# One order for all loads behind the first batch's q and k, and two of its value copies moved to GpSimd

## The chip, the cores and the metric

The kernel runs on one core of one Trainium2 chip. The metric is the device time of one execution in microseconds (us), the median of several runs. The core has five engines that work side by side: TensorE (PE in the profile, with its weight loads as PEld), VectorE (DVE), ScalarE (ACT), GpSimd (POOL) and SyncE (SP). DMA engines carry the loads; here nearly all loads are issued from GpSimd's queue and the stores from SyncE's.

## What is computed

Sliding-window causal attention (window 64) over 8 batches, 8 heads, 576 positions and head size 64, followed by a two-layer feed-forward with SiLU:

```python
scores = scale * np.matmul(q, k.transpose(0, 1, 3, 2))
mask = (rel >= 0) & (rel < window)            # rel = i - j, window = 64
attn = softmax(np.where(mask, scores, -1e9))
attn_out = np.matmul(attn, v)                 # (8, 8, 576, 64)
x = attn_out.transpose(0, 2, 1, 3).reshape(4608, 512)
h = x @ w_in                                  # (512, 2048)
out = (h / (1 + exp(-h))) @ w_out             # (2048, 512)
```

Inputs and output are float32 in memory; the kernel computes in bfloat16 with float32 sums.

## The kernel before

**Attention.** A batch is done in three groups `g` of three windows of 64 queries. Each window sees 128 keys: its own block of 64 and the one before. Batch 0 is done in six units (three groups for each half `a` of the heads), the later ones in three units each. A unit is: scores on TensorE (`scores_first` for batch 0, L315 and L323, `scores` for the others, L335), exponentials on ScalarE (`expo`, L341), for later batches a mask on VectorE (`masking`, L344), the product with the values on TensorE (`values`, L353), then on VectorE the reciprocal of the sums (`inverse`, L360), the norm (`normal`, L363) and a transposition into `bridge` (`to_bridge`, L367), the tile from which the feed-forward reads.

**Loads.** Batch 0's q and k come in whole pairs of heads (`natb`, L234 and, for the first pair, L237) and are transposed on TensorE. For the other batches `load_rows` (L244) takes one head's q or k in a load of 72 KB, four to a buffer, and `turn_blocks` (L251) transposes a buffer on VectorE. `load_v` (L260) brings the values of two blocks of all heads, or of the last one; it fills the odd windows `n` of `vv`. The even ones are filled by `shift_v` (L301 and L303), which copies 64 partitions up or down, two copies for each of four parts. `load_w_in` (L263) brings w_in in ten pieces (four with 256 columns, six with 512, in pairs for the two halves `a` of the rows), `load_w_out` (L269) w_out in eight pieces of 256 rows.

**Feed-forward.** Nine tiles of 512 tokens. The first layer (`first_layer`, L373) goes through 16 weight tiles `ft` of 128 columns with four matmuls each, ScalarE applies SiLU (`silu`, L379), and the second layer (`second_layer`, L385) sums over the 16 in four banks of 128 tokens; `copy_out` (L391) and `store` end it. Tile 0 is special: its first layer takes 576 tokens, all of batch 0. For the first `THIRDS` weight tiles it works in widths of 192, one for each group of batch 0 (classes `in0`, `in1`, `in2`), so that it can begin when the first group is normed; for the others in widths of 256 and 320. Its second layer goes weight tile by weight tile, so that it needs w_out piece by piece. `rest_of_first` (L382) carries its last 64 tokens to tile 1. In tile 1 the first `SPLIT` weight tiles are done in two widths (192 and 256), the others in one (448). The score and value groups of a later batch are put between the matmuls of the second layer.

**What sets the order.** The class `Plan` runs a list of queues, one for each class of work (`dma`, `shift`, `norm`, ...). Each has a rank (tables `rank`, `rank0` for batch 0, `ahead` for its first group, `also`); a lower number goes first. `Plan.run` walks through time with a planned duration for each operation, and whenever an engine is free lets it take the head of the best queue whose inputs are ready. The order found in this way is written out as the program of each engine. All loads but batch 0's q and k are in the class `dma`, so they are issued from GpSimd in the order in which they were added: before, batch 0's values, all of w_in, then batch 1's q and k rows, w_out pieces and values in the order of `SECOND_LOADS`. A planned duration is not a measured one: on the chip each instruction waits for the semaphores of what it reads, and an engine goes through its program in order. GpSimd's loads use eight semaphores in turn, so a load waits for the landing of the one eight places before it.

While nothing can be done yet, TensorE runs filler matmuls on a blank tile (`warm`, L605).

Of the kernel before, what the change touches and what calls it, by code (L numbers as in the profile page):

```python
# [122 lines left out]
def kernel(ctx, tc, q, k, v, w_in, w_out, out):  # L123
# [14 lines left out]
    NN, NNB, NE, NOT, NGT = 8, 8, 12, 4, NFT + 3  # L138
    THIRDS, SPLIT, SECOND_LOADS = 4, 16, "0w12w3wvwvwvwvvww"
    FIRST_LOADS = [(x[0], int(x[1])) for x in "q0 k0 q1 k1 q2 q3 k2 k3 v0 v1 v2 v3 v4".split()]  # L140
    NOX, NRC, NV = 6, 6, 3
# [3 lines left out]
    def SHIFT(b, m, hf):  # L145
        return {"DVE": 0.31, **({"ACT": 0.64} if m > 1 else {})}
    scale = 1.0 / float(D) ** 0.5
# [34 lines left out]
        rank=dict(prime=-8, early=-10, one=-9, edge=-8.5, first=-9, dma=-1, ld0=-1, dma0=-8.7, st=-2, silu=-3, silu_in0=-3.1, silu_in1=-3.1, silu_in2=-3.1, silu_in3=-3, silu_next=-3, out=-2, pv=0, s=1, in0=96, in1=97, in2=98, in3=98.5, out0=98.7, next=98.9, moe=99, warm=200, turn=2,  # L182
                  norm=0, inverse=0, bridge=0, exp=1, mask=1, lift=2, block=2, shift=2, shift2=2, cast=4, rest=3, late=5, clear=9),
        rank0=dict(turn=-6, cast=-6, lift=-5, shift=-4.5, shift2=-4.05, exp=-4, mask=-4, inverse=-3.5, norm=-3, bridge=-3.2),
        ahead=dict(s=-6.5, exp=-4.6, pv=-5.5, inverse=-4.3, norm=-4.2, bridge=-4.25),
        also=dict(inverse1=-4.2, norm1=-4.1, bridge1=-4.15),
    )
# [230 lines left out]
    def add_first_batch():  # L418
        got = {}
        for what, u in FIRST_LOADS:  # L420
            if what == "v":
                add_v_loads(0, [u], [c_vv[0]])
                continue
            kk = "qk".index(what)
# [22 lines left out]
    def add_w_out(which):  # L447
        wout.extend(p.add("dma", {"POOL": 0.75}, lambda _, f=f: load_w_out(f), dma=1.29, lat=MARGIN) for f in which)

    def add_batch_qk(b):  # L450
        busy = s_last.get(b - NK, []) + ([c_k[b % NK]] if b < NK else [])
        for what in SECOND_LOADS if b < NIV else "0123":
            if what == "w":
                add_w_out([len(wout)])
            elif what == "v":
                add_v_loads(b, [len(v_landed.get(b, []))], [c_vv[b]])
            else:
                add_four(b, *divmod(int(what), 2), busy)

    def add_four(b, a, kk, busy):  # L460
        i = n_nat[0] % NN
        n_nat[0] += 1
        ld = [p.add("dma", {"POOL": 0.6}, lambda _, h=h: load_rows(i, b, a, kk, h), nat_free.get(i, []),
                    dma=0.42, lat=MARGIN) for h in range(4)]
        nat_free[i] = [p.add("block", {"DVE": 0.79}, lambda _, part=part: turn_blocks(i, b, a, kk, part),
                             ld + busy, b=b) for part in range(2)]
        kq_done[(b, a)] = kq_done.get((b, a), []) + nat_free[i]

    def add_v_loads(b, parts, busy):
        v_landed.setdefault(b, []).extend(  # L470
            p.add("dma", {"POOL": 1.0 if m < NPAIR else 0.75}, lambda e, m=m: load_v(e, b, m), busy,
                  dma=(0.95 if m < NPAIR else 0.5), lat=MARGIN * (b > 0)) for m in parts)

    def add_batch_v(b):
        busy = pv_last.get(b - NV, []) + [c_vv[b % NV]]
        if b >= NIV:
            add_v_loads(b, range(NPAIR + 1), busy)
        lv = v_landed[b]
        for g in range(NG):
            v_done[(b, g)] = lv[:g + 2] if g < 2 else list(lv)  # L480
        for m, z in ([(i, i + 1) for i in range(NPAIR)] if b < NIV else [(0, NPAIR)]):
            for hf in range(2):
                sh = p.add("shift" if b or 2 * m + hf < 3 else "shift2", SHIFT(b, m, hf) if b == 0 else {"DVE": 0.1 + 0.17 * (z - m)}, lambda e, hf=hf, m=m, z=z: shift_v(e, b, hf, m, z),
                           lv[m:z], b=b)
                for g in range(NG):
                    if any(3 * g <= n < 3 * g + 3 for n in range(2 * m + 2 * hf, 2 * z + 2 * hf, 2)):
                        v_done[(b, g)] = v_done[(b, g)] + [sh]
# [110 lines left out]


    add_first_batch()  # L600
    add_batch_v(0)


    def warm(op):
# [4 lines left out]
                 pool="all")  # L609
    for lo, hi in ((0, 256), (256, 512), (512, 1024), (1024, 1536), (1536, 2048)):  # L610
        landed = [p.add("dma", {"POOL": 0.6}, lambda _, a=a, lo=lo, hi=hi: load_w_in(a, lo, hi), dma=1.31 * (hi - lo) / 512)
                  for a in range(2)]
        win.extend([landed] * ((hi - lo) // 128))
    add_batch_attention(0)
# [4 lines left out]
    for b in range(1, B):  # L619
        add_batch_qk(b)  # L620
        add_batch_v(b)
        if b == 1:
            add_w_out(range(len(wout), 8))
        while TB * (n_tile + 1) <= b * NB:
            add_tile(n_tile)
            n_tile += 1
        add_batch_attention(b)
# [34 lines left out]
```

## Time and profile before

| what | value |
|---|---|
| median of 4 runs | 299.7 us (299.35 to 300.49) |
| the profiled execution | 300.49 us, span in the profile 298.7 us |
| TensorE busy | 290.8 us, 97% of the span, 3667 matmuls |
| ScalarE, VectorE, GpSimd busy | 177.1, 137.8, 118.9 us |
| granted TensorE clock | 1.00 throughout |
| DMA packets | 28.64 MB, mean 96 GB/s |

The span is what the profiler saw from the first instruction to the last; the time of a run is a little longer. "Busy" counts an engine's own instructions, on GpSimd also the time in which it writes the descriptors of a load (the `DMA_DIRECT2D` rows). In the timeline a row gives start, duration, engine, line, operation and count, and in brackets how long the engine was idle before and what ended that; "issue" there means that the profile shows nothing that it waited for. In the list of waits a row is engine, line, what it waited for, and the total, the number and the longest of the waits.

### The profile page before, as it was taken

The numbers are of one execution on the slowest core, as the hardware profiler recorded it, in microseconds if no ns is written. First come the engines' busy times: TensorE is split into PE (matmuls) and PEld (weight loads), VectorE is DVE, ScalarE is ACT, GpSimd is POOL, SyncE is SP. The second block draws the span as 40 slices with busy tenths as digits, with TensorE's granted clock in tenths as the row PEclk, the third lists the DMA queues.
The fourth block names the chain that finished last, engine by engine and source line by source line (L and its number), as shares of the span: only waits on it lengthen the run. The fifth ranks groups of instructions, "written<-read, shape, count | busy, mean of one in ns | idle before, by whom it ended". The sixth has DMA issues, their size and how long they took to land.

```text
span 298.7 us, 8593 instructions
## 1 busy us (share of the span) xinstructions
PE 290.8 (97%) x3667; PEld 151.4 (51%) x3667; DVE 137.8 (46%) x338; ACT 177.1 (59%) x348; POOL 118.9 (40%) x183
## 2 busy tenths in 40 slices
PE   8989979999999999999999999999999999999996
PEld 4568634885444544454444544454444544444444
DVE  4862448959985479327931692066006600000000
ACT  4888654886376745675477537753876376226511
POOL 8976976969999989953200000000000000000000
PEclk9999999999999999999999999999999999999999
DMA  8999999999999999986900210011001100011012
GB/s 165 173 188 166 138 170 163 226 135 135 170 183 143 128 186 178 150 82 104 122 0 1 72 53 22 2 41 68 35 2 37 72 35 3 35 70 37 0 70 71
DMA packets 83110, 28.64 MB, mean 96 GB/s; under 512 B 72576, under 2 KB 78336, under 8 KB 83072
## 3 DMA queue, kind: packets, MB, share of 16 engines
q0 software_dynamic: 77312, 18.07, 65.5%
q1 hardware_dynamic: 5760, 10.03, 9.4%
q8 instruction: 28, 0.46, 0.6%
q14 instruction: 10, 0.08, 0.1%
HBM read 36.70 MB, written 9.44 MB: 154 GB/s over the span
## 4 chain that ended last, share of the span: by engine, by line
PE 82%; DMA 8%; POOL 6%; DVE 1%; issue 1%; ACT 1%; ACTq 0%; POOLq 0%
PE mp L385 39%; PE mp L373 33%; PE at L373 3%; DMA nat<-in_q_dram 3%; PE at L335 3%; PE mp L353 3%; DMA w_out_sb<-in_moe_w_out_dram 2%; DMA vv<-in_v_dram 2%; POOL nat L244 2%; POOL vv L260 1%; POOL natb L234 1%; POOL w_in_sb L263 1%; ACT e L341 1%; POOL w_out_sb L269 0%; DVE e L344 0%
## 5 line engine op out<-in xcount | busy, mean ns | idle before, releaser
L385 PE MATMUL mp<-w_out_sb,g 128*128 128x512 bf16 (+2 forms) x608 | 130.5, 369 | 1.6 <-DMA w_out_sb<-in_moe_w_out_dram 1.6
L373 PE MATMUL mp<-bridge,w_in_sb 128*128 128x512 bf16 (+3 forms) x552 | 113.0, 357 | 1.4 <-issue 1.1
L373 PEld LDWEIGHTS <-w_in_sb 128*128 128x128 bf16 x720 | 68.2, 97 | 59.8 <-issue 6.7
L379 ACT ACTIVATE g<-mp 128x512 bf16<-128x512 f32 (+3 forms) x138 | 74.8, 556 | 27.8 <-PE mp L373 27.6
L385 PEld LDWEIGHTS <-g 128*128 128x128 bf16 x608 | 55.7, 98 | 61.4 <-issue 1.1
L391 ACT COPY ot<-mp 128x512 f32<-128x512 f32 (+2 forms) x36 | 20.1, 562 | 62.6 <-PE mp L385 46.5
L344 DVE TENSOR_TENSOR e<-e,mask 128x384 bf16<-128x384 bf16 x84 | 25.7, 348 | 52.2 <-ACT e L341 51.8
L341 ACT ACTIVATE e<-at 128x384 bf16<-128x384 f32 x89 | 36.8, 496 | 17.4 <-PE at L335 17.1
L260 POOL DMA_DIRECT2D vv<-in_v_dram x40 | 33.9, 869 | 10.6 <-PE mp L353 6.6
L244 POOL DMA_DIRECT2D nat<-in_k_dram x56 | 34.6, 628 | 7.5 <-DMA nat<-in_q_dram 2.2
L244 POOL DMA_DIRECT2D nat<-in_q_dram x56 | 34.1, 630 | 5.5 <-DMA vv<-in_v_dram 1.6
L367 DVE STREAM_TRANSPOSE bridge<-ox 128x384 bf16<-128x384 bf16 x48 | 24.8, 552 | 0.0
L251 DVE STREAM_TRANSPOSE qt<-nat 128x576 bf16<-128x576 bf16 x28 | 20.7, 790 | 5.7 <-DMA nat<-in_q_dram 5.6
L251 DVE STREAM_TRANSPOSE kt<-nat 128x576 bf16<-128x576 bf16 x28 | 20.6, 785 | 3.9 <-DMA nat<-in_k_dram 3.9
L373 PE MATMUL at<-bridge,w_in_sb 128*128 128x256 bf16 (+2 forms) x168 | 20.2, 267 | 0.0
L363 DVE TENSOR_TENSOR ox<-mp,rc 128x384 bf16<-128x384 f32 x37 | 18.3, 535 | 0.1
L379 ACT ACTIVATE g<-at 128x256 bf16<-128x256 f32 (+2 forms) x42 | 15.3, 373 | 1.9 <-PE at L373 1.0
L353 PEld LDWEIGHTS <-e 128*32 128x32 bf16 x1152 | 11.0, 95 | 10.5 <-issue 5.5
L360 DVE RECIPROCAL rc<-mp 128x6 f32<-128x6 f32 x37 | 7.1, 194 | 18.2 <-PE mp L353 17.4
L303 DVE COPY vv<-vv 64x512 bf16<-64x512 bf16 (+1 forms) x13 | 6.5, 498 | 12.5 <-DMA vv<-in_v_dram 12.3
L335 PEld LDWEIGHTS <-kt 32*128 32x128 bf16 x1008 | 9.3, 92 | 5.4 <-issue 3.4
L335 PE MATMUL at<-qt,kt 32*128 32x64 bf16 x1008 | 11.6, 190 | 0.0
(56 smaller groups left out, 111.5 us busy)
## 6 DMA issues: line engine op xcount, KB each, us to landing
out_dram<-ot SPq DMA_DIRECT2D x35, 256.0 KB, 2.1
vv<-in_v_dram POOLq DMA_DIRECT2D x32, 128.0 KB, 5.1
nat<-in_q_dram POOLq DMA_DIRECT2D x56, 72.0 KB, 3.8
nat<-in_k_dram POOLq DMA_DIRECT2D x56, 72.0 KB, 3.9
w_out_sb<-in_moe_w_out_dram POOLq DMA_DIRECT2D x8, 256.0 KB, 7.3
w_in_sb<-in_moe_w_in_dram POOLq DMA_DIRECT2D x6, 256.0 KB, 7.2
vv<-in_v_dram POOLq DMA_DIRECT2D x8, 64.0 KB, 5.1
w_in_sb<-in_moe_w_in_dram POOLq DMA_DIRECT2D x4, 128.0 KB, 5.6
```

Source lines behind the costliest of these rows:

```text
L244: nc.gpsimd.dma_start(out=nats[i][32 * h:32 * h + 32].rearrange("p (m x) -> p m x", m=NB), in_=(q, k)[kk][b, 4 * a + h].rearrange("(m p r) ...
L251: nc.vector.transpose(out=to[:, (2 * a + part) * S:(2 * a + part + 1) * S].rearrange("x (m t r) -> x m r t", t=32, r=2), in_=nats[i].rearr ...
L260: queue[e].dma_start(out=vv[b % NV][r, :, n, 0:D], in_=v[b][:, 128 * m:128 * m + r.stop - r.start].rearrange("h p d -> p h d"))
L335: nc.tensor.matmul(at_six(op["bank"][h])[:, a, x], lhsT=kt[b % NK][r, at:at + 128], rhs=qt[b % NK][r, at:at + 64], start=(s == a == x == 0 ...
L341: nc.scalar.activation(out=es[n % NE], in_=at_six(bank), func=ACTF.Exp, scale=scale)
L344: nc.vector.tensor_mul(es[n % NE], es[n % NE], mask0 if g == 0 else mask)
L353: nc.tensor.matmul(at_pv(bank)[32 * h:32 * h + 32, x, t], lhsT=e_of(b, a, n, h)[:, x, 32 * t:32 * t + 32], rhs=vv[b % NV][:, 4 * a + h, 3 ...
L367: nc.vector.transpose(out=bridge[:, n0:n0 + 3, 2 * a:2 * a + 2].rearrange("x t s (u i) -> x t s u i", u=2), in_=oxs[n % NOX].rearrange("p ...
L373: nc.tensor.matmul(banks[bank["bank"][0]][:, 0:hi - lo], lhsT=w_in_sb[:, c, ft * 128:(ft + 1) * 128], rhs=bridge[:, (j * TT + lo) // 64:(j ...
L379: nc.scalar.activation(out=gts[gt][:, lo:hi], in_=banks[bank["bank"][0]][:, 0:hi - lo], func=ACTF.Silu)
L385: nc.tensor.matmul(banks[bank["bank"][0]][:, 0:hi - lo], lhsT=gts[gt][:, m * 128:(m + 1) * 128], rhs=w_out_sb[:, f, lo:hi], start=(f == 0) ...
L391: copies[e](out=ots[ot][:, lo:hi], in_=banks[bank["bank"][0]][:, 0:hi - lo])
```

## The change

There are four parts.

1. All loads behind batch 0's q and k are added in one list, `SECOND_LOADS`: `V` and `v` are a part of batch 0's and batch 1's values, `i` a piece of w_in, `r` one head's rows of batch 1's q or k, `w` a piece of w_out. Batch 1's rows stand among w_in's pieces, two w_in pieces stand ahead of the last parts of batch 0's values, and w_out follows behind most rows.
2. Of batch 0's eight `shift_v` copies the sixth and the eighth go to GpSimd, the other six to VectorE. Before, VectorE or ScalarE could take the last four; VectorE took two of those and ScalarE the other two. The last three copies are a class of their own, `shift3`.
3. In batch 0, the reciprocals, norms and bridges of the second group are ranked later (-4.0 to -3.98, before -4.2 to -4.1), behind those of the first group for both halves of the heads.
4. `THIRDS` is 6 and not 4, `SPLIT` 12 and not 16. Planned durations of the value loads change a little.

GpSimd's program becomes, behind batch 0's q and k: v, v, w_in, v, w_in, v, v, w_in, row, w_in, shift, w_in, shift, w_in, three rows with a w_in piece among them, and so on. On TensorE the last two score groups of batch 0 now come before the second value group, and the second layer of tile 0 does 9 matmuls, not 17, before batch 1's first scores.

```diff
-    THIRDS, SPLIT, SECOND_LOADS = 4, 16, "0w12w3wvwvwvwvvww"
-    FIRST_LOADS = [(x[0], int(x[1])) for x in "q0 k0 q1 k1 q2 q3 k2 k3 v0 v1 v2 v3 v4".split()]
+    THIRDS, SPLIT, SECOND_LOADS = 6, 12, "VViViVViriiirrirriirrrrriwrrrrrrwwwvvvwwvwvw"
+    FIRST_LOADS = [(x[0], int(x[1])) for x in "q0 k0 q1 k1 q2 q3 k2 k3".split()]
...
     def SHIFT(b, m, hf):
-        return {"DVE": 0.31, **({"ACT": 0.64} if m > 1 else {})}
+        return {"POOL": 0.7} if 2 * m + hf == 5 or 2 * m + hf == 7 else {"DVE": 0.31}
...
-        rank0=dict(turn=-6, cast=-6, lift=-5, shift=-4.5, shift2=-4.05, exp=-4, mask=-4, inverse=-3.5, norm=-3, bridge=-3.2),
+        rank0=dict(turn=-6, cast=-6, lift=-5, shift=-4.5, shift2=-4.05, shift3=-3.9, exp=-4, mask=-4, inverse=-3.5, norm=-3, bridge=-3.2),
         ahead=dict(s=-6.5, exp=-4.6, pv=-5.5, inverse=-4.3, norm=-4.2, bridge=-4.25),
-        also=dict(inverse1=-4.2, norm1=-4.1, bridge1=-4.15),
+        also=dict(inverse1=-4.0, norm1=-3.98, bridge1=-3.99),
...
+    IN_PIECES = [(a, lo, hi) for lo, hi in ((0, 256), (256, 512), (512, 1024), (1024, 1536), (1536, 2048)) for a in range(2)]
+
+    def add_loads(order):
+        pieces, rows = iter(IN_PIECES), []
+        for what in order:
+            if what == "i":
+                add_w_in(*next(pieces))
+            elif what == "w":
+                add_w_out([len(wout)])
+            elif what in "Vv":
+                b = "Vv".index(what)
+                add_v_loads(b, [len(v_landed.get(b, []))], [c_vv[b]])
             else:
-                add_four(b, *divmod(int(what), 2), busy)
+                rows = rows or row_loads(1)
+                rows.pop(0)()
...
-                sh = p.add("shift" if b or 2 * m + hf < 3 else "shift2", ...
+                sh = p.add("shift" if b or 2 * m + hf < 3 else "shift2" if 2 * m + hf < 5 else "shift3", ...
...
     add_first_batch()
+    add_loads(SECOND_LOADS)
     add_batch_v(0)
...
-    for lo, hi in ((0, 256), (256, 512), (512, 1024), (1024, 1536), (1536, 2048)):
-        landed = [p.add("dma", {"POOL": 0.6}, lambda _, a=a, lo=lo, hi=hi: load_w_in(a, lo, hi), dma=1.31 * (hi - lo) / 512)
-                  for a in range(2)]
-        win.extend([landed] * ((hi - lo) // 128))
```

`row_loads(1)` makes the list of batch 1's 16 row loads, each followed, after the fourth of a buffer, by its two VectorE transposes; `add_w_in` adds one piece and notes for which weight tiles it is needed.

## The prediction

> **What bounds the kernel now.** I read the page's totals first, then who waited for whom on TensorE, then busy time by window, then the transfers of the stretch that looked thin, and last the chain of waits. Page and waits:
> ```profile
> PE 290.8 (97%) x3667; PEld 151.4 (51%) x3667; DVE 137.8 (46%) x338; ACT 177.1 (59%) x348; POOL 118.9 (40%) x183
> PE mp L385 <- DMA w_out_sb<-in_moe_w_out_dram: 1.6, 2, 1.0
> PE mp L373 <- issue: 1.1, 1, 1.1
> PE at L353 <- ACT g L382: 0.6, 1, 0.6
> ```
> TensorE is busy 97% of the span. What a load order can win is the few microseconds it idles, and they lie before 51 us. By windows (us, then PE, PEld, DVE, ACT, POOL busy, clock, DMA share, GB/s):
> ```profile
> 17.00:20.93 3.93, 2.82 (x42) 2.66 (x33) 3.03 (x9) 2.65 (x9) 2.61 (x5) 1.00 1.20 198
> 20.93:34.02 13.09, 13.09 (x116) 10.70 (x114) 4.97 (x9) 11.17 (x29) 9.78 (x17) 1.00 1.32 154
> 34.02:54.05 20.03, 17.78 (x312) 8.59 (x310) 12.00 (x36) 9.74 (x28) 15.27 (x23) 1.00 1.51 162
> ```
> Window 1 is the first 32 matmuls of tile 0's first layer, window 2 its rest, window 3 tile 0's second layer with three score and three value groups of batch 1 (the last value group was run a little later; it is counted in). Windows 1 and 3 hold 1.11 and 2.25 us of idle PE, window 2 none; the clock is full. Next PE's timeline (start, us) around the idle spots, and the rate of all transfers from 25 to 38 us in 40 slices:
> ```profile
> 19.00 0.41 PE L373 MATMUL mp<-bridge,w_in_sb 128*128 128x192 bf16 x3
> 20.53 0.24 PE L373 MATMUL mp<-bridge,w_in_sb 128*128 128x192 bf16 x1 [1.11 <-issue]
> 38.64 0.38 PE L385 MATMUL mp<-w_out_sb,g 128*128 128x512 bf16 x1 [0.97 <-DMA w_out_sb<-in_moe_w_out_dram]
> 41.75 1.89 PE L385 MATMUL mp<-w_out_sb,g 128*128 128x512 bf16 x8 [0.64 <-DMA w_out_sb<-in_moe_w_out_dram]
> GB/s 183 190 203 190 208 179 173 144 103 80 129 139 88 136 140 125 123 136 144 84 46 19 38 110 151 205 196 175 173 194 164 156 166 161 166 166 137 149 134 180
> ```
> The stream falls from about 190 GB/s to 80-144 between 27.3 and 31 us, and to 19-46 near 32 us. At 170 GB/s that is some 1.8 us of lost transfer, and w_out pieces 2 and 3 come late by about as much. Its cause is in the chain:
> ```profile
> 17.32 9.36 DMA nat<-in_q_dram
> ...
> 27.60 2.38 POOL nat L244 x4
> 29.98 0.74 POOL w_out_sb L269
> 30.72 2.41 POOL nat L244 x4
> ```
> Batch 1's 16 row loads go out in one block at 0.60 us of GpSimd each, while their landings, when queued, come about 0.42 us apart: the queue runs dry. W_in pieces of 256 KB cost 0.70 us to issue and 1.31 us to land (six landings in 7.86 us).
>
> **The change, part by part.** The prices (landing spacings, from issue plus time to landing of single loads): v 0.85, its half load 0.4, w_in's 128 KB piece 0.66, its 256 KB piece and w_out's 1.3, a row load 0.42 (0.26 to 0.64). The profiled run took 300.49 us for a span of 298.7; the median of four runs is 299.7. I sum against 300.49 and shift by 0.8.
>
> *PE's work* hardly changes. Four matmuls 192 wide take 0.33 us, 256 wide 0.435, 320 wide 0.545: 0.0035 us fixed each. Tile 0 gets 8 more matmuls, tile 1 has 16 fewer: 0.03 us.
>
> *Start of the first layer.* V part 3 landed at 14.25 before. Two 128 KB pieces of w_in now go ahead of it: 14.25 + 2 x 0.66 = 15.6. VectorE has one shift (0.29) waiting for it in the middle of the chain for the first groups: 15.6 + shift 0.3 + norm 0.55 + reciprocal 0.1 + bridge 0.5 = 17.05, against 17.01 before. Behind that shift, on VectorE, stand all the norms and bridges that PE waits for. ScalarE loses two copies of 0.62 us, so its last exponentials end near 15.5, not 16.66, and the table load of 1.28 follows earlier; PE then waits for VectorE anyway, so this is worth nothing alone.
>
> *GpSimd's two shifts.* No GpSimd copy is in the trace. Lower end: VectorE's 0.29. Upper end: the 128x128 affine select at 0.33 scaled to 512 columns, 1.32. Value: the step between the 128x64 and 128x128 selects (0.27 to 0.33) carried on, 0.7. Queued behind them on GpSimd are all later loads: the second shift waits for v part 3 (15.6), ends at 16.3, and piece 5 of w_in is issued then instead of at 13.13. A w_out piece on a nearly empty queue took 4.74 us to land: 21.0. Before, the 33rd matmul, the first to need piece 5, started at 20.93. With norms taken first group first, the middle group's bridge ends 2.1 us after 17.05 (twice a norm 0.47, a reciprocal 0.11 and a bridge 0.47 from start to start), and 32 matmuls end at 20.3; PE then waits for piece 5 or, as before, for its instructions. So this stage is even, and its cover of 0.7 us is the slack between 20.3 and 21.0; beyond it each microsecond is paid.
>
> The Trainium skill speaks against this part: SBUF — State Buffer, "Who interferes with whom", has VectorE copies in a two-port mode and GpSimd exclude each other for a whole instruction. In both places a VectorE shift and a GpSimd shift are freed by the same landing, so by that rule one waits for the other, VectorE up to 0.7 us; the first layer would start at 17.7 and the sum of this stage would still be near 21. No row of this trace shows that pairing.
>
> *Order of w_in and rows.* The last w_in piece landed at 25.14. Now ten row loads stand ahead: 25.14 + 10 x 0.42 = 29.3, plus the 1.1 us that the landing right after 25.14 came late in the trace (26.68), plus 0.4 for the bubble behind the shifts: 30.8. With rows at 0.26 and no late landing 28, at 0.6 32.6. PE needs it four weight tiles before the first layer's end: 34.0 - 4 x 0.98 = 30.1, the third matmul at 30.3. So I take a wait of 0.5 and an end at 34.6 (34.0 if covered).
>
> *Order of w_out.* After 30.8: piece 0, six rows, pieces 1 to 3 (5.2 + 2.5) end at 38.5. PE asks for piece 1 at 34.6 + 1.7 = 36.3 (it lands at 35.9), for piece 2 at 38.6 (37.2), for piece 3 at 40.8 (38.5). The rows are in at 34.6 and the last transposes (1.5) done at 36.1, when scores want them at 36.5. Batch 1's v parts 0 and 1 land at 39.4 and 40.2 and are shifted by 41; the first value group comes at 34.6 + 29 x 0.217 + two scores 1.0 = 41.9. After the third v part piece 4 lands at 42.4, or 43.1 with one landing late by 0.7 as piece 2 was before; wanted at 34.6 + 32 x 0.217 + two scores and one value group 1.5 = 43.1. The waits of 0.97 and 0.64 go; what is late next is piece 4, with no margin.
>
> *The sum.* The work of window 3 is 17.78 us: 34.6 + 17.78 = 52.4 if nothing waits. I keep the 0.65 us before a value group, which no load caused: 53.0 against 54.05, a gain of 1.0; with w_in's last piece covered 1.6. I take 1.3. After 54 us the order is the same work on a full PE, so the gain reaches the end: 300.5 - 1.3 = 299.2, by the median 298.4.
>
> The 1.11 us idle "issue" comes just after one 16 KB packet of the instruction queue ran for 0.96 us in the full stream (18.06); the next lag may fall anywhere, so I move nothing for it. The skill's page Runtime: NRT & Kernel Launch, "Instruction fetch mechanics", calls such a refill mostly hidden; by that the 1.11 would be something else and could go, which would put the time near 297.5. The row has the idle time, and the sum keeps it.
>
> **Rivals.**
> *The waits only move* (C). GpSimd loses 1.4 us to copies and up to 0.9 waiting for v part 3, and the stream dries there instead of at 32 us. For it: POOL busy 9.78 of 13.09 us in window 2, so little is spare. Against it: the pieces then issued are long. Price: the lost 1.8 comes back; 299.7, from 299.1 to 300.4.
> *Slower: w_in becomes the bound* (B). Window 2 had no idle microsecond because all of w_in was in by 25.14. If rows cost their issue time of 0.6 each, the last piece lands at 32.6, PE stands 2.3 us in the first layer, which ends at 36.3, and 36.3 + 17.78 + 0.65 = 54.7: 0.7 slower. With the GpSimd copies at 1.32 the stream is later by 1.2 more: 1.9 slower. That is 300.4 to 301.6, say 300.9. It decides once the last w_in piece lands after about 32. For it: rows once came 0.64 apart. Against it: 0.26 to 0.48 elsewhere.
> *The change does not do what it says*: excluded; the changed program's instruction order has the rows among w_in, the two copies on GpSimd, none on ScalarE.
>
> **How the numbers follow.** The likeliest case (A) has 0.62: 298.4, from 297.3 (of 3.4 us of idle PE in windows 1 and 3 all but 1 us gone) to 299.1. C has 0.18, B 0.20. 0.3% is 0.9 us, what a measurement of this kernel can tell from no change. Of A 0.55 lies below 298.8 and 0.07 above; C gives 0.02 faster, 0.12 same, 0.04 slower; B 0.01 same, 0.19 slower. Faster 0.57, same 0.20, slower 0.23. The range 297.0 to 300.8 leaves out the slow half of B and a tip of A.
>
> **What would show it.** Right: no PE wait for w_out at L385 and no dip under 100 GB/s near 32 us; rows all landed by 35 us; tile 1's first layer starting 1 to 1.5 us earlier. Wrong: PE at L373 waiting for w_in beyond 1 us after 25 us (B); GpSimd copies over 1.3 us or a first layer starting after 17.8; the w_out waits still there with a dry stretch at 16 to 21 us (C).

## The result, and the profile after

The changed kernel takes 300.56 us (median of 43 runs, 299.26 to 307.65); the kernel before, run beside it on the same chips, 299.48 us (64 runs). The ratio is 1.0046, 95% interval 1.0036 to 1.0056: slower by 1.1 to 1.7 us, where 1.3 us of gain were forecast. Disturbed runs, such as the one of 307.65, are left out of the ratios.

The profiled execution after took 300.51 us for a span of 298.7 us, as before. That the two profiled runs agree misleads: 300.51 is typical of the changed kernel, and 300.49 lies 1.0 us above the median of the kernel before. So the kernel before was profiled twice more (b1, b2 below), and those two, with spans of 297.8 and 297.9 us, are the ones to compare with.

Page and list of waits after (total, number and longest of the waits, in us):

```profile
PE 289.5 (97%) x3656; PEld 149.7 (50%) x3656; DVE 138.6 (46%) x338; ACT 175.8 (59%) x344; POOL 120.4 (40%) x185
PE at L373 <- DMA w_in_sb<-in_moe_w_in_dram: 1.9, 1, 1.9
PE mp L353 <- DVE vv L303: 1.6, 1, 1.6
PE at L353 <- issue: 0.8, 1, 0.8
PE at L373 <- DVE bridge L367: 0.6, 1, 0.6
```

The two waits for w_out at L385 are gone, as forecast. In their place PE stands 1.9 us for w_in in the first layer, which did not happen before, and 1.6 us before the last value groups.

The windows of the three stages (us; PE, PEld, DVE, ACT, POOL busy; clock, DMA share, GB/s): the start of tile 0's first layer, the rest of that layer, and the second layer with batch 1's groups. The first window ends some eight matmuls further on in the layer than the one before the change did.

```profile
17.33:21.74 4.41, 3.64 (x47) 3.14 (x40) 4.41 (x12) 2.64 (x8) 4.41 (x8) 1.00 1.21 152
21.74:36.34 14.60, 12.75 (x116) 10.47 (x114) 5.07 (x10) 11.02 (x29) 10.95 (x17) 1.00 1.36 163
36.34:54.74 18.40, 17.59 (x354) 8.47 (x352) 13.12 (x39) 9.61 (x27) 14.10 (x22) 1.00 1.51 166
```

Window 2, which held no idle PE before, now holds 1.85 us; window 3 shrank from 20.03 to 18.40 us. The second layer starts at 36.34 us, against 34.02 in the given profile and 33.26 and 33.32 in b1 and b2. What the second layer wins, 1.63 us, was lost before it began: its start is 2.3 us later than in the given profile and 3.0 to 3.1 later than in b1 and b2.

PE's and GpSimd's timelines after (start, us) at the places that carry this:

```profile
16.61 0.37 PE L353 MATMUL mp<-vv,e 128*32 128x65 bf16 x24 [1.56 <-DVE vv L303]
32.63 0.28 PE L373 MATMUL at<-bridge,w_in_sb 128*128 128x256 bf16 x1 [1.85 <-DMA w_in_sb<-in_moe_w_in_dram]
14.50 0.64 POOL L301 COPY vv<-vv 64x512 bf16<-64x512 bf16 x1 [1.31 <-DMA vv<-in_v_dram]
15.09 0.69 POOL L263 DMA_DIRECT2D w_in_sb<-in_moe_w_in_dram  x1
15.78 0.62 POOL L301 COPY vv<-vv 64x512 bf16<-64x512 bf16 x1
16.33 0.71 POOL L263 DMA_DIRECT2D w_in_sb<-in_moe_w_in_dram  x1
```
Before the change GpSimd's issues stood closer (the given profile):

```profile
9.63 4.20 POOL L263 DMA_DIRECT2D w_in_sb<-in_moe_w_in_dram  x6
14.54 2.79 POOL L263 DMA_DIRECT2D w_in_sb<-in_moe_w_in_dram  x4 [0.71 <-DMA vv<-in_v_dram]
```

The chain after:

```profile
7.99 6.37 DMA vv<-in_v_dram
...
26.00 6.58 DMA w_in_sb<-in_moe_w_in_dram
32.63 0.94 PE at L373 x6
```

GpSimd, the engine that issues all these loads, stands still for 1.31 us until part 2 of batch 0's values is in (14.36), because its first copy waits for that; then it copies for 1.26 us in two pieces. Pieces 4 and 5 of w_in (counted from 0, as in the prediction) are issued at 15.09 and 16.33 us, against 12.43 and 13.13 before (the fifth and sixth of the row at 9.63, 0.70 each), and the last, piece 9, at 26.00. It lands at 32.59.

What that does to the stream of loads shows in the window from 15 to 20 us (last column GB/s): first the kernel before (b1), with the next window, then the changed one.

```profile
15.00:20.00 5.00, 4.13 (x105) 3.35 (x104) 5.00 (x15) 4.77 (x12) 3.93 (x7) 1.00 1.22 189
20.00:25.00 5.00, 5.00 (x50) 4.34 (x48) 1.32 (x5) 4.36 (x13) 2.57 (x4) 1.00 1.32 181
```
```profile
15.00:20.00 5.00, 2.66 (x95) 2.27 (x92) 4.90 (x15) 3.31 (x8) 5.00 (x9) 1.00 1.11 145
20.00:25.00 5.00, 5.00 (x59) 4.76 (x59) 2.76 (x8) 4.57 (x14) 4.22 (x8) 1.00 1.31 162
```

189 GB/s before, 145 after, and from 20 to 25 us 181 and 162: some 0.3 MB less, or 1.7 us of stream at 185 GB/s.

### The profile page after: what moved, and what is told of

The parts are those of the page before. It is cut to its first block, busy times and chain, and to the rows that moved or that the text cites. A ratio compares the mean times of both kernels' runs of the same rounds, so it can differ in the third digit from the quotient of the medians.

```text
span 298.7 us, 8572 instructions
## 1 busy us (share of the span) xinstructions
PE 289.5 (97%) x3656; PEld 149.7 (50%) x3656; DVE 138.6 (46%) x338; ACT 175.8 (59%) x344; POOL 120.4 (40%) x185
## 4 chain that ended last, share of the span: by engine, by line
PE 88%; DMA 6%; POOL 4%; issue 1%; ACT 0%; POOLq 0%; ACTq 0%
PE mp L385 43%; PE mp L373 35%; PE at L335 3%; PE at L373 3%; PE mp L353 3%; DMA w_in_sb<-in_moe_w_in_dram 2%; DMA vv<-in_v_dram 2%; DMA nat<-in_k_dram 2%; POOL natb L234 1%; POOL w_in_sb L263 1%; POOL nat L244 1%; POOL vv L260 1%; PE at L353 1%; POOL vv L301 0%; POOL ident L193 0%
## 5 line engine op out<-in xcount | busy, mean ns | idle before, releaser
L385 PE MATMUL mp<-w_out_sb,g 128*128 128x512 bf16 (+2 forms) x608 | 130.3, 369 | 0.0
L373 PEld LDWEIGHTS <-w_in_sb 128*128 128x128 bf16 x712 | 67.1, 97 | 61.8 <-issue 6.0
L379 ACT ACTIVATE g<-mp 128x512 bf16<-128x512 f32 (+3 forms) x141 | 75.8, 555 | 26.4 <-PE mp L373 26.0
L385 PEld LDWEIGHTS <-g 128*128 128x128 bf16 x608 | 55.8, 98 | 60.8 <-issue 0.2
L391 ACT COPY ot<-mp 128x512 f32<-128x512 f32 (+2 forms) x37 | 20.7, 563 | 61.2 <-PE mp L385 42.3
L341 ACT ACTIVATE e<-at 128x384 bf16<-128x384 f32 x90 | 37.3, 497 | 17.6 <-PE at L335 17.4
L244 POOL DMA_DIRECT2D nat<-in_k_dram x56 | 34.6, 627 | 5.8 <-DMA vv<-in_v_dram 1.6
L373 PE MATMUL at<-bridge,w_in_sb 128*128 128x192 bf16 (+3 forms) x148 | 18.7, 271 | 2.6 <-DMA w_in_sb<-in_moe_w_in_dram 1.9
L363 DVE TENSOR_TENSOR ox<-mp,rc 128x384 bf16<-128x384 f32 x39 | 19.2, 533 | 0.0
L379 ACT ACTIVATE g<-at 128x192 bf16<-128x192 f32 (+3 forms) x37 | 13.7, 389 | 5.8 <-PE at L373 5.4
L353 PE MATMUL mp<-vv,e 128*32 128x65 bf16 x936 | 11.2, 194 | 1.6 <-DVE vv L303 1.6
L303 DVE COPY vv<-vv 64x512 bf16<-64x512 bf16 (+1 forms) x14 | 7.3, 524 | 10.3 <-DMA vv<-in_v_dram 7.5
```

Of the source, the lines that this page charges most:

```text
L244: nc.gpsimd.dma_start(out=nats[i][32 * h:32 * h + 32].rearrange("p (m x) -> p m x", m=NB), in_=(q, k)[kk][b, 4 * a + h].rearrange("(m p r) ...
L341: nc.scalar.activation(out=es[n % NE], in_=at_six(bank), func=ACTF.Exp, scale=scale)
L353: nc.tensor.matmul(at_pv(bank)[32 * h:32 * h + 32, x, t], lhsT=e_of(b, a, n, h)[:, x, 32 * t:32 * t + 32], rhs=vv[b % NV][:, 4 * a + h, 3 ...
L373: nc.tensor.matmul(banks[bank["bank"][0]][:, 0:hi - lo], lhsT=w_in_sb[:, c, ft * 128:(ft + 1) * 128], rhs=bridge[:, (j * TT + lo) // 64:(j ...
L379: nc.scalar.activation(out=gts[gt][:, lo:hi], in_=banks[bank["bank"][0]][:, 0:hi - lo], func=ACTF.Silu)
L385: nc.tensor.matmul(banks[bank["bank"][0]][:, 0:hi - lo], lhsT=gts[gt][:, m * 128:(m + 1) * 128], rhs=w_out_sb[:, f, lo:hi], start=(f == 0) ...
```

## The experiments

All times are medians in us; "before" is the kernel before on the same chip in the same session.

| run | edit | time | before | ratio, 95% interval |
|---|---|---|---|---|
| e1 | after, copies on VectorE and ScalarE | 300.50 | 299.64 | 1.0037 (1.0019 to 1.0056) |
| e2 | after, rows behind w_in | 305.34 | 299.64 | 1.0149 (1.0107 to 1.0190) |
| e3 | after's code, before's loads and copies | 300.50 | 299.64 | 1.0040 (1.0020 to 1.0059) |
| e4 | before, w_out pieces spaced out | 301.96 | 299.64 | 1.0069 (1.0042 to 1.0096) |
| e5 | before, 6 and 12 for 4 and 16 | 299.99 | 299.48 | 1.0006 (0.9983 to 1.0030) |
| e6 | after, 4 and 16 for 6 and 12 | 302.04 | 299.48 | 1.0083 (1.0054 to 1.0112) |
| e7 | before, ranks of the change | 299.46 | 299.58 | 0.9996 (0.9972 to 1.0020) |
| e8 | e1 with the values first | 298.69 | 299.58 | 0.9964 (0.9936 to 0.9991) |
| e9 | e1 with w_in whole | 301.25 | 299.58 | 1.0057 (1.0030 to 1.0085) |
| e10 | values first, rows late | 302.92 | 299.58 | 1.0095 (1.0060 to 1.0130) |
| e11 | after with the values first | 301.53 | 299.54 | 1.0056 (1.0036 to 1.0076) |
| e12 | before with the values late | 300.82 | 299.54 | 1.0047 (1.0025 to 1.0069) |
| e13 | e8, all copies on VectorE | 300.01 | 299.54 | 1.0011 (0.9992 to 1.0031) |

### The copies taken off GpSimd (e1)

```diff
-        return {"POOL": 0.7} if 2 * m + hf == 5 or 2 * m + hf == 7 else {"DVE": 0.31}
+        return {"DVE": 0.31, **({"ACT": 0.64} if m > 1 else {})}
```

> The changed kernel with its load order kept, but the two shift copies back on VectorE or ScalarE, so that GpSimd only issues loads. Theory COPIES (the two GpSimd copies and their waits for v parts 2 and 3 hold the load queue from 13.2 to 16.4 us, the stream falls from 184 to 145 GB/s between 15 and 20 us, and that is what makes the last w_in piece late): pieces 4 and 5 of w_in are issued near 13 and 14 us instead of 15.1 and 16.3, the last piece lands near 30.6 instead of 32.6, TensorE's wait for it at L373 falls from 1.85 to under 0.5 us, and the time from 300.5 to about 299. Theory ROWS (the ten row loads ahead of the last pieces are enough by themselves): the last piece still lands after 31.8, the wait stays above 1 us, the time above 300.

W_in's last piece lands at 30.1 us, not 32.59, and nothing waits for it: with the copies off GpSimd the lateness is gone. But the time stays at 300.50. PE's list of waits in this run:

```profile
PE mp L373 <- DVE bridge L367: 2.0, 2, 1.3
PE at L373 <- DMA w_in_sb<-in_moe_w_in_dram: 1.2, 1, 1.2
```

The first layer now starts at 15.43, after a wait of 0.73 for a bridge; then it stands 1.30 for the next bridge and 1.21 for w_in's piece 5. Its 33rd matmul is at 22.04 and the second layer starts at 35.14, still 1.8 us later than in b1 and b2. So something else holds the front. Three of its runs had full clock throughout, and they too took 300.27 to 300.58.

### Batch 1's rows behind w_in (e2)

```diff
-"VViViVViriiirrirriirrrrriwrrrrrrwwwvvvwwvwvw"
+"VViViVViiiiiiiirrrrrrrrrrwrrrrrrwwwvvvwwvwvw"
```

> The changed kernel with the two GpSimd copies kept, but batch 1's ten rows that stood among w_in's pieces moved behind the last of them. Both theories: the last w_in piece lands ten rows of 0.42 us earlier, near 28.4, and TensorE's wait at L373 goes. ROWS: nothing else was wrong, so the time falls by the whole 1.85 to about 298.7. COPIES: the 2 us that the stream lost at 15 to 20 us are still lost, all rows still land near 36.4, the transposes end near 38, and TensorE, which is there at 36.5, waits for them ahead of batch 1's first scores by about 1.5 us: time about 300.2.

305.34, the slowest of all. With the copies on GpSimd the stream runs at 107 GB/s from 15 to 20 us even without a row in it; w_in's piece 5 lands at 22.5 (PE waits 1.80), and w_out now comes late as well (2.17 at 41.9). Five of its six runs, the profiled one too, had stages of half clock, so the number is too high by a few us; the one run at full clock took 302.07. Moving the rows alone is no cure.

### What the rest of the change costs (e3, e5, e7, e6)

E3 keeps the changed code but gives it before's loads and copies; e5 and e7 put single parts of that rest into the kernel before; e6 takes the widths out of the changed one.

```diff
# e3, in the changed kernel (and SHIFT as in e1)
+"VVVVViiiiiiiiiirrrrwrrrrrrrrwrrrrwvwvwvwvvww"
# e5, in the kernel before; e6 the reverse in the changed one
-    THIRDS, SPLIT = 4, 16
+    THIRDS, SPLIT = 6, 12
# e7, in the kernel before
-        also=dict(inverse1=-4.2, norm1=-4.1, bridge1=-4.15),
+        also=dict(inverse1=-4.0, norm1=-3.98, bridge1=-3.99),
```

> The changed kernel with the load order of before and the copies back on VectorE or ScalarE: what is left of the change is 6 and 12 for 4 and 16, the ranks of the second group's norms and the planned durations of the value loads. Both theories: the time of before within 0.3%, about 299.5, with before's two waits for w_out. A rival, REST: the smaller widths or the new ranks cost by themselves, then it is slower than before by 0.5 us or more.

> The kernel before with 6 and 12 for 4 and 16 as its only edit: loads, copies and ranks are those of before. The rest of the change took 300.50 against 299.64 by itself, so the load order and the copies seem to come out even. Theory WIDTHS: the loss is in the two numbers (weight tiles 4 and 5 are wanted in width 192 before the last group is there, so pieces 4 and 5 of w_in are asked for 0.7 us earlier; tile 1 has four weight tiles that start only when all its tokens are there): about 300.4. Theory RANKS: the loss is in the later norms of the second group or in the value loads' planned durations: 299.6, no change.

> The kernel before with one table line of the change: the second group's reciprocals, norms and bridges of batch 0 ranked at -4.0 to -3.98. In the program this takes one of ScalarE's two shift copies to VectorE (seven there, one left on ScalarE) and puts the first value groups of the other half ahead; in the changed kernel the same line alters no instruction, with its copies on GpSimd or not. RANKS (what the change's code costs with the loads in the old order is this line): the first layer starts at 17.5 or later and the time is 300.3 to 300.6, a ratio of 1.003 to 1.004. PLANNED LOADS (it is the planned durations of the value loads instead): 299.5, the same as before.

> The changed kernel with 4 and 16 for 6 and 12 as its only edit; GpSimd's program is the same. WIDTHS: the time falls by what the two numbers cost, from 300.5 to about 299.6 or below. RANKS: no change, 300.5. Under both the last w_in piece still lands near 32.6 and TensorE still waits for it by about 1.8 us, because GpSimd's program is the same.

The widths alone change nothing that can be measured (1.0006), nor do the ranks (0.9996): both theories that laid a loss on them fall. In e3 the widths stand together with the two things that are left, other planned durations (of the value loads and of w_in's pieces) and the class `shift3`, and this rest costs about as much as the whole change (1.0040). The new ranks have no part in it: in e3, as in the changed kernel and in e1, e8, e9 and e11, the old ranks give the same program, instruction for instruction. The profile of e3, of a run 0.85 us above its median, has a wait of 1.0 for ScalarE's copy, 1.1 for w_out and 0.6 for the bridge of tile 1, each after a different order of the planner; which of the parts it is stays open. The changed kernel and e1, e8, e9 and e11 all carry this rest, so it does not enter the differences between them. In the changed kernel the new widths help: with 4 and 16 it takes 302.04, and its profile, of a run 1.2 us above that, waits 1.6 and 1.2 us for w_in pieces 5 and 9. That it does so because fewer narrow matmuls fill the time until they land is argued, not shown.

### The kernel before, twice more, and its w_out waits (b1, b2, e4)

> The kernel before, unchanged, for a second profile of it. The profile of before took 300.49 us, a full 1.0 above the median of its many later runs (299.48), while the profile of the changed kernel (300.51) is at its median (300.56): the two traces show no difference because before's was a long one. If so, this execution is nearer 299.5 and has less idle TensorE before 51 us than the 3.5 us of the first profile; theory FETCH: what is missing are waits with no releaser (the 1.11 us at the instruction fetch at 20.5); theory STREAM: it is the 1.6 us of waits for w_out.

> The kernel before, unchanged, for a third profile, so that a typical chain of waits can be told from a chance one. As for the second: near 299.5, idle TensorE before 51 us below 3.5 us; FETCH and STREAM differ in which waits are missing.

> The kernel before with one w_out piece behind each four rows, instead of one behind the first four, one behind twelve and one behind sixteen; nothing else is changed by hand. If the dry stretch near 32 us comes from the block of rows that are issued at 0.60 us each, as the prediction had it, a long piece in each gap keeps the stream fed: no rate under 80 GB/s near 32 us, w_out pieces 2 and 3 land 2 us earlier or more, TensorE's waits of 0.97 and 0.64 us at L385 go, and the time falls by about 1 to 298.4. If the stream is no faster for it, the rows land a piece (1.3 us) later, the wait moves to the first scores, and the time stays at 299.5 or above.

```diff
# e4, in the kernel before
-"0w12w3wvwvwvwvvww"
+"0w1w2w3wvwvwvwvvw"
```

B1 took 299.58 us, b2 299.63. Both have the waits for w_out (0.95 and 0.79; 0.99 and 0.76), so those are no accident. The 1.11 us "issue" at the 33rd matmul is: none in b1, 0.56 in b2, and by its size it can be most of the 1.0 us by which the given profile is long.

Nor do the waits come from the dip to 19-46 GB/s near 32 us, to which the prediction put them down. In b1 the same 40 slices from 25 to 38 us never fall below 88 GB/s (in b2 the lowest is 43), and b1 waits for w_out longer than the given profile, 1.9 us for 1.6:

```profile
PE mp L385 <- DMA w_out_sb<-in_moe_w_out_dram: 1.9, 3, 1.0
```

In e4 w_out's third and fourth pieces land 3.0 and 2.4 us earlier than in b1 and the waits for w_out fall to 0.7; but the planner puts 25 instead of 17 second-layer matmuls ahead of batch 1's first scores, the bridges of batch 1 come later, and PE waits 1.4 us for one in tile 1's first layer. That is the fastest of its six runs (300.37); what the others, at 301.4 to 303.5, lose on top is not shown. Spacing out w_out is worth nothing by itself.

### Values first (e8), w_in whole (e9)

```diff
# e8, on e1 (with before's ranks)
-"VViViVViriiirrirriirrrrriwrrrrrrwwwvvvwwvwvw"
+"VVVVViiiriiirrirriirrrrriwrrrrrrwwwvvvwwvwvw"
# e9, on e1
+"VViViVViiiiiiiirrrrrrrrrrwrrrrrrwwwvvvwwvwvw"
```

> The changed kernel with the shift copies on VectorE and ScalarE as before, and all five parts of batch 0's values ahead of w_in; batch 1's rows stay among w_in's pieces. FRONT (the changed order loses because values wait behind w_in pieces, so that the bridges end late): the first layer starts at 16.9, the 33rd matmul at 20.2, w_in's last piece lands at 30 to 30.5, the second layer starts at 33.5 to 34 and no w_out wait is left: 298.3 to 299.0. MIDDLE (rows ahead of w_in's last pieces cost it): PE waits 1 to 2 us for w_in near 30 us, and the time stays at 300.2 to 300.8. BYTES (up to some 50 us PE needs w_in, rows and w_out about as fast as they come, whatever the order, and a wait taken out at one place comes back at another): 299.4 to 300.2 with 1.5 to 2.5 us of waits for loads somewhere before 52 us.

> The changed kernel with the shift copies on VectorE and ScalarE as before, the values behind two w_in pieces as in the change, but all of w_in ahead of batch 1's rows. FRONT: the start stays at 15.4 with waits of about 2 us for bridges, the second layer starts at 35, the time is 300.3 to 300.8. MIDDLE: no wait for w_in after 22 us, the second layer starts at 33.5 to 34, 299.3 to 299.7. BYTES: w_in's last piece lands near 26, w_out's second piece and batch 1's rows come late instead, with waits of 1 to 2 us between 34 and 45 us; 299.6 to 300.5.

E8 takes 298.69 us, the only version that beats both kernels (0.9964, interval up to 0.9991). FRONT had the time right and the steps only in part: the first layer starts at 17.59, not 16.9, since a value group waits for ScalarE's copy, the last w_in piece and the second layer come 0.4 and 0.6 us after its ranges, and a wait of 0.5 for w_out is left.

```profile
PE at L353 <- ACT vv L301: 1.0, 1, 1.0
PE at L373 <- DMA w_in_sb<-in_moe_w_in_dram: 0.5, 1, 0.5
PE mp L385 <- DMA w_out_sb<-in_moe_w_out_dram: 0.5, 1, 0.5
```
```profile
15.00:20.00 5.00, 3.83 (x122) 2.87 (x106) 4.67 (x13) 4.72 (x11) 4.60 (x7) 1.00 1.34 180
```

The stream is back at 180 GB/s, the last w_in piece lands at 30.9, the second layer starts at 34.63 and tile 1's first layer at 52.65. In b1 that is 52.56, with a value group of some 0.5 us still to come, so about 0.4 us is won there; the rest of the 0.9 us between the medians comes in tiles 1 and 2. E9, which keeps the values late and clears the rows out of w_in instead, takes 301.25, more than e1 and than any theory had: w_in is in by 25.0, but the first layer stands for bridges, 1.22 us before its start and then 1.30 and 0.65. (The profile is of a run of 302.27 with a stage of half clock, and it also waited 1.0 us for a load of q before the first layer.) MIDDLE falls, and BYTES too: E8 shows that 0.9 us were to be had.

### The four combinations (e11, e12)

```diff
# e11, in the changed kernel
-"VViViVViriiirrirriirrrrriwrrrrrrwwwvvvwwvwvw"
+"VVVVViiiriiirrirriirrrrriwrrrrrrwwwvvvwwvwvw"
# e12, before's widths, ranks, copies and later loads
+"VViViVViiiiiiiirrrrwrrrrrrrrwrrrrwvwvwvwvvww"
```

> The changed kernel with one list altered: all five parts of batch 0's values ahead of w_in, GpSimd's two copies kept. VALUES (the place of the values carries the loss): GpSimd no longer stands 1.3 us for value part 2, w_in's last piece lands before 31.5, the second layer starts at 34.5 to 35, 298.5 to 299.2. COPIES (1.3 us of copies in the load queue matter as much): w_in's sixth and last pieces come late as in the changed kernel, PE waits 1.5 us or more for them, 299.8 to 300.5.

> The kernel before with one piece of its order altered: two 128 KB pieces of w_in ahead of parts 2 and 3 of batch 0's values; the later loads, widths, ranks and shift engines as before. VALUES: the first layer starts early with some 2 us of waits for bridges and the second layer starts at 35 or later: 300.3 to 301.2. COPIES or MIDDLE: 299.5 to 299.9.

E11 takes 301.53: COPIES had it, though with too good a time. GpSimd still stands for value parts 2 and 3 (0.51 and 0.43) and copies for 1.31, with fewer pieces issued ahead of that, and the three pieces behind the copies go out from 14.58 on. Its windows and waits:

```profile
15.00:20.00 5.00, 3.69 (x135) 3.33 (x127) 4.97 (x15) 4.17 (x11) 5.00 (x9) 1.00 0.92 105
20.00:25.00 5.00, 3.18 (x24) 2.46 (x23) 0.78 (x2) 1.85 (x6) 3.23 (x5) 0.80 1.29 157
```
```profile
PE at L373 <- DMA w_in_sb<-in_moe_w_in_dram: 1.8, 2, 1.1
PE at L373 <- DVE bridge L367: 1.1, 1, 1.1
```

The stream falls to 105 GB/s and w_in pieces 4 and 5 land at 21.4 and 22.8. The 0.80 in the clock column is a stage of half clock from 23.0 to 26.4, which followed these waits; eight of its twelve runs had none, and they too took 300.31 to 301.89.

E12 takes 300.82: with the copies, ranks, widths and later loads of before, and two 128 KB pieces of w_in ahead of the values' last parts, it is 1.3 us slower than the kernel before (0.6 to 1.4 in the three of twelve runs that kept full clock). How much of that is the two pieces alone is not shown: e12 is the changed code and keeps its planned durations and `shift3`, and e3, with these and the new widths, lost 0.9. All of w_in is in by 25.2 in e12, and in the first layer PE stands for bridges alone:

```profile
15.33 0.33 PE L373 MATMUL mp<-bridge,w_in_sb 128*128 128x192 bf16 x2 [0.34 <-DVE bridge L367]
16.95 0.32 PE L373 MATMUL mp<-bridge,w_in_sb 128*128 128x192 bf16 x2 [1.30 <-DVE bridge L367]
21.13 0.32 PE L373 MATMUL at<-bridge,w_in_sb 128*128 128x192 bf16 x2 [1.66 <-DVE bridge L367]
```

By the four combinations there are two faults, and either seems enough for the whole loss:

| | copies on GpSimd | copies on VectorE and ScalarE |
|---|---|---|
| values behind w_in pieces | 300.56 (the change) | 300.50 (e1) |
| values first | 301.53 (e11) | 298.69 (e8) |

Undoing either alone wins nothing; undoing both wins 1.9 us. E8 has the old ranks, but they alter no instruction in any of the four. Each combination is planned anew, though, so PE's order differs a little too: in e1 three value groups of batch 0 come behind the first 13 matmuls of the first layer, in the other three ahead of them.

The times stand, on 12 runs or more each. How the loss is made up is less sure, since each profile shows one run. The changed kernel, e1 and e11 each have, besides the waits named above, one gap of 0.81, 0.96 and 0.73 us with the releaser "issue" at the same place of PE's program, near 50 us; e8's profile has none there. Of the 1.5 us between the spans of the profiles of e1 and e8 (298.5 and 297.0) up to 0.96 is that gap. Whether it belongs to those programs or to chance, one profile of each cannot say (see the last section).

### Which engine copies, and rows spread thinner (e13, e10 and e14)

```diff
# e13, on e8
+        return {"DVE": 0.31}
# e10 and e14, on e8
+"VVVVViiiiiiiirrirrirwrrrwrrrwrrrwrrvwvvwvwvw"
```

> The version with values first and all eight shift copies on VectorE, none on ScalarE or GpSimd. Its predecessor lost 0.99 us before a value group that waited for ScalarE's copy. If that wait is simply gone: 297.7 to 298.4. If VectorE's two more copies (0.29 each) delay the bridges of the next groups by as much: 298.5 to 299.0.

> A version meant to beat both: values first, copies on VectorE and ScalarE as before, eight w_in pieces at once, the last two among the first five rows, then one w_out piece to every three rows, so that the queue always has a long load in it. FRONT and MIDDLE agree on it: the first layer starts at 16.9, w_in is all in by 28, the second layer starts at 33.3, and the w_out waits of 0.97 and 0.7 go: 298.0 to 298.8. BYTES: the waits shift to later w_out pieces or batch 1's values (1 to 1.5 us before 52 us), 299.2 to 299.8.

> The same kernel as the version with rows late in w_in, for a second profile. If its time is one wait for batch 1's last bridges in tile 1 (2.37 us in the first profile) that is longer in most runs: 302.5 to 303.3 with 4 to 5 us there. If it is a half-speed clock stage: the granted clock shows 0.5 for some 3.4 us and the wait stays at 2.4.

E13: 300.01, 1.3 us worse than e8 and worse than both expectations. The wait of 0.99 for ScalarE is gone, but VectorE's two more copies stand between the bridges, and the first layer, which starts at 15.00, waits at once for the next one:

```profile
17.41 0.33 PE L373 MATMUL at<-bridge,w_in_sb 128*128 128x192 bf16 x2 [2.08 <-DVE bridge L367]
```
```profile
16.19 0.56 DVE L303 COPY vv<-vv 64x512 bf16<-64x512 bf16 x1
```

E10 was meant to beat both and takes 302.92. No wait for w_out is left, as wished. But the last rows land at 37.3 and 37.8 us instead of 34.4, batch 1's first scores begin at 40.4 instead of 36.7, and the planner puts the last value group into tile 1's first layer, where PE then stands for its bridge:

```profile
PE at L373 <- DVE bridge L367: 2.4, 1, 2.4
```

This is in both profiles. The first (300.67) was its fastest run; the second, e14 (302.87), has 1.57 us more before a value group at 114.8. E14's expectation had two readings, a longer wait here or a stage of half clock, and neither came: the wait is 2.4 again and the clock is full. The rows are not only filler for the stream. In these profiles no score waits for a row on the chip: the planner, which takes the rows to come later, puts 28 second-layer matmuls ahead of batch 1's first scores, where e8 has 8 or 9, and so batch 1 comes late.

## Why the prediction was wrong, step by step

- **Start of the first layer**: 17.05 forecast, 17.33 measured. Value part 3 landed at 15.5 (15.6 forecast); VectorE's shift began at 15.98 and took 0.57 instead of 0.3. Right to 0.3 us; but set beside 17.01, where b1 and b2 start at 16.70 and 16.87. With 17.05 for 17.01 the step also put the place of the values, behind two w_in pieces, at nothing. The edits of e1 and e8 differ in that place alone (the ranks alter nothing) and the two are 1.8 us apart, so this is a second term that was priced wrong; it shows only with the copies off GpSimd, since with them on it values first wins nothing (e11).
- **GpSimd's two shifts**: 0.64 and 0.62 for the 0.7 taken, piece 5 issued at 16.33 and landed at 21.3 for 16.3 and 21.0. All four numbers held. What failed is the sentence "so this stage is even": the 33rd matmul starts at 21.07, as at 20.93 in the given profile, but against 20.2 in b1 and b2 0.8 to 0.9 us were lost. The given run hid them under its issue stall of 1.11, which the sum carried along on both sides; in the profile after, it did not come at this place, but one of 0.81 came at 49.53.
- **Order of w_in and rows**: the step that failed. The last piece was put at 30.8 and landed at 32.59; a wait of 1.85 for 0.5, and a second layer at 36.34 for 34.6. The mis-sized term is "plus 0.4 for the bubble behind the shifts". With the copies off GpSimd the same rows in the same order let the last piece land at 30.1 (e1) and 30.9 (e8), as forecast; the bubble is 1.7 to 2.5 us. This step took 0.4 us for all that GpSimd loses; it loses 1.31 us for value part 2 and 1.26 in the copies, with only four pieces of w_in on their way, and only the price of rival C had such a loss in it. That the copies and their waiting cause the bubble is shown by e1 and e8; that the lateness of the piece alone costs the 1.1 us is not, since e1, without it, is as slow.
- **Order of w_out**: right that the waits for w_out go; piece 4 lands in time. That window 3 is 18.40 for 18.43 forecast is in part luck: the wait of 0.65 for ScalarE that the sum kept is gone, and the gap of 0.81 at 49.53 stands in its place. One reading was off: before the change the 16 row loads do not all go out in one block. Seven go one or two at a time from 17.32 on, and only the last nine, with a w_out piece among them, stand from 26.97 to 33.1. The rows are in by 36.4, not 35.
- **The sum**: "After 54 us the order is the same work" was nearly so: from the end of window 3 to the last matmul of the first layer it is 227.17 us (281.91 - 54.74) against 227.83 before (281.88 - 54.05). This 0.66 makes the two given profiles equal; where it comes from beyond 0.4 in tiles 1 and 2 stays open. Against b1, whose window 3 ends at 53.05, the change is 1.7 us behind at 54.74 and makes up 0.8 of it by the end: against b1 and b2 (280.98, 281.02) the last first-layer matmul ends 0.9 later, and the medians differ by 1.1.
- **The rivals**: B's numbers came: it had the last piece at 32.6, the first layer's end at 36.3, tile 1 at 54.7 and a time from 300.4; measured are 32.59, 36.34, 54.74 and 300.56. Its sign, PE waiting for w_in beyond 1 us after 25 us, came too. The agreement is luck, for its reason did not hold: it took the rows to land 0.6 us apart, and where they stand in a row they land 0.42 to 0.57 apart; with the same rows in the same order the last piece is in at 30.1 and 30.9 (e1, e8). What made it late is the dry stretch at 16 to 21 us that C named.
- **The rule on the shared ports** (the Trainium skill, SBUF — State Buffer, "Who interferes with whom"): VectorE's copy began 0.20 us after GpSimd's of 0.62 and took 0.57 us instead of 0.29. By the rule it would have stood for the 0.42 still to run and taken 0.71, an estimate, and the prediction's full size of it put the first layer at 17.7; measured is 17.33. That GpSimd's copy is behind the 0.28 more is not shown: the same copy took 0.56 in e13 and 0.50 and 0.52 in b1 with no copy on GpSimd, only descriptor writing.

The forecast of 298.4 was near what this version gives with the copies off GpSimd and the values first (e8, 298.69). Both faults lie in front of the part that it summed with care, and the prediction had priced both there, one at nothing and one at 0.4 us. How the loss divides between the waits shown and the "issue" gap near 50 us stays open.

## What to carry to other kernels

An engine that issues the loads should neither compute nor wait while the stream is needed: in this kernel 1.31 us of waiting and 1.26 us of copies on it brought the last w_in piece 1.7 to 2.5 us later, because what it would have issued is what keeps the stream full. With that engine free, loads that open a chain over several engines (here the values: shift, value product, norm, bridge) were better put ahead of loads that one engine needs later, even though the later ones are short (e8 against e1). When undoing one part of a change brings nothing, undo two: faults that overlap can hide one another. And the profile of one run has its own accidents; the stall of 1.11 us in the given one was as large as the effect in question, and two more profiles of the same kernel showed it. Profile the version after more than once too.

## What the runs showed of the hardware that was not expected

**Half clock after short waits.** In several versions the granted clock falls to one half for 3.4 us (e11: 23.0 to 26.4; e9: 17.9 to 21.4), after PE had stood for 0.7 and 1.1 us within 2.2 us, or 1.2 and 1.3 within 3. Versions with such pairs of waits early in the first layer show it in many runs (e1 and e12 9 of 12, e9 8, e13 5, e11 4, e2 5 of 6), the changed kernel, whose waits of 1.56 and 1.85 lie 16 us apart, in 6 of 44, e3, e5, e7 and e8 in none of 12. Pairs are not the whole condition: e4 (2 of 6), e6 (4 of 11) and e10 (6 of 10) have it too, and the profiles of e4 and e10 show one long wait in tile 1, of 1.4 and 2.4 us, and no such pair. What exactly lowers the clock is not shown. The Trainium skill (TensorE: Matmul & The Clock Gate, "Part 1: The HAM clock gate (the "warmup" mystery)") has the clock fall after an idle window of about 3.4 us; the length of the stage agrees, but here PE had not been idle for a whole one. E9's runs with such a stage took 301.80 in the median, those without 300.94: in e9 the stage costs 0.9 us on top of the waits.

**Instruction stalls at fixed places.** PE's longer "issue" gaps fall in 11 of the 18 profiles at one of the same two places of its program, 768 instructions apart, and vary from nothing to 1.25 us in programs that are nearly the same; in the kernel before, at the first place, they were 1.11, 0 and 0.56 us in three runs of one program. So they move a single run by as much as this change did. At the second place, near 50 us, the profiles of the changed kernel, e1, e2, e7, e9, e11, e12 and e13 have one of 0.73 to 1.25 us, those of the other versions none. That part of it comes with a version, and so is a price of the change, is not ruled out: no version but the kernel before was profiled unchanged more than once with one of these gaps in it.
